# Attention tile: transposed probabilities ahead of the first half of the scores, sink transpose behind it

## The chip, the cores and the metric

The kernel runs on one core of a Trainium2 chip. Its time is the device time of one execution in microseconds (us); lower is better. The core has five engines that run their own instruction queues in order and meet only at semaphores: TensorE (PE; its weight loads are listed apart as PEld), VectorE (DVE), ScalarE (ACT), GpSimd (POOL) and SyncE (SP), which here only starts DMA transfers.

## The reference

Windowed attention with sink keys is followed by a two-level mixture of experts. Batch 4, 8 heads, sequence 768, head width 64, 4 sink keys, window 128; 4 groups of 4 experts with hidden width 1024.

```python
scores = scale * np.matmul(q, k.transpose(0, 1, 3, 2))
keep = is_sink | in_window
scores = np.where(keep, scores, -1000000000.0)
a = np.exp(scores - np.max(scores, axis=-1, keepdims=True))
a = a / (np.sum(a, axis=-1, keepdims=True) + 1e-09)
x = np.matmul(a, v)                       # then reshaped to 3072 x 512
...
g_idx = np.argmax(x @ w_group, axis=1)    # group of a row, then expert in the group
...
h = np.maximum(xg[mask_e] @ w1[g, e], 0.0)
out[tok_idx] = combined[:, None] * (h @ w2[g, e])
```

## The kernel before

All work is written out in program order. `Pinned` (lines 108 to 117) keeps every engine's instructions in the order in which the Python code issues them, so the order of the calls in the loop is the order in each queue; semaphores between the engines follow from which tile an instruction reads and writes. Most instructions are recorded under line 101, the wrapper's, so the profile's rows are told apart by tile names.

**Stages.** The loop of lines 1081 to 1161 runs over i = 0 to 25. It handles 24 attention tiles of 128 query rows (six per batch; t = i mod 6 is the position in the sequence) as a pipeline of three stages. In iteration i, tile i gets its scores, maxima and exponentials; tile a = i - 1 gets its probabilities transposed and multiplied with the values; tile b = i - 2 is brought back to rows, normalized and stored, and its routing logits are computed. Between these lie pieces of the routing (which row goes to which expert) and, from the middle on, the first weight tiles of the experts. After the loop comes the expert stage, matmul after matmul over eleven groups of experts.

**One iteration, PE's queue.** `scores(i, g)` (line 710) fills PSUM tile `ps0` or `ps1` (g = 0 or 1, four heads each) from the keys `kb` and the queries `qb` with 16 matmuls, 64x216, or 64x144 for t = 0. `trans(a)` (line 764) transposes tile a's probabilities `pt` into `tp` with 16 matmuls, heads 0 to 7 in order, each waiting for its own head's exponentials. `sink_t(a)` (line 783) transposes the sink keys' probabilities `sp` with two matmuls, into a part of the PSUM tiles `lg` and `po`. `logits(b)` writes `lg`, `natural(b)` writes `tp`, `values(a, 0)` and `values(a, 1)` add into `po` in four groups of 16 matmuls (`pu` with the previous block's values, then `pa`, for each half of the heads), and `sink_values(a)` adds four more.

**The other queues.** ACT copies `tp` to `pa` (`evac`, line 771, one call for each half of the heads) and `sink_t`'s output to `spT` (`sink_evac`, line 789, two casts), then runs the eight exponentials of `exps(i, 0)` and `exps(i, 1)`, which write `pt`, and at the end `out_evac`, which copies `po` to `xT`. POOL cuts each half of `pa` to the window with two `affine_select` instructions (into `pu` and back into `pa`), four for an iteration, none for t = 0; after the exponentials it makes `sp` (`sink_split`, line 757: two casts and a subtraction). DVE does `maxima(i, g)` (for t > 0 a `copy_predicated` on `ps`, then four fused reductions that give `sm` and `st`), `norm(b)` (reads `tp`, writes `xt`, which SP stores), routing work, and the lower parts `wlo` of the weights. `tp` has one buffer: `trans(a)` of an iteration waits for `norm` of the iteration before. SP starts the store of `xt`, then the next iteration's `vv` (values), then `qb` and `kb` of tile i + 2 after `scores(i, 1)`.

Iterations 0 and 1 fill the pipeline: iteration 1 issues both halves of the scores first, and `warm` adds small matmuls on `lg` after the scores in iterations 0 to 2 (8, 10 and 6). Iterations 24 and 25 have no scores.

Of the kernel before, what the change touches and what calls it, by code (L numbers as in the profile page):

```python
# [130 lines left out]
def moe_attention(tc, kqT, vN, vS, nsw, wgx, w1, w2, out):  # L131
    nc = Pinned(tc)
    v = nc.vector
    with ExitStack() as top, ExitStack() as att:
# [39 lines left out]
        def pair():  # L174
            return ps_p.tile([P, 2, 4 * P], F32, name="tp")

        def warm(k, dst=None):
            dst = pair()[:, 0, 0:192] if k and dst is None else dst
            for _ in range(k):
                nc.tensor.matmul(dst, wz[:, 0:P], wz, start=True, stop=True)  # L180
# [23 lines left out]
        def load_v(i):  # L204
            b, t = divmod(i, NT)
            vts[i] = wk.tile([P, 2, DM], F32, name="vv", bufs=3)
            nc.sync.dma_start(vts[i].rearrange("p f n -> p (f n)"), vN[b, t])
# [15 lines left out]
        def issue():  # L223
            if jobs:
                load(jobs.pop(0))
# [112 lines left out]
        def put_gates(n):  # L338
            for _ in range(min(n, len(gates))):
                t, g = gates.pop(0)  # L340
                nc.sync.dma_start(xd[t * P:(t + 1) * P, DM:XW], g)
# [292 lines left out]
        def gather(r, j):  # L634
            w = min(P, CAPT[r] - j * P)
            cc = BASE[r] + j
            xg[r, j] = t = gp.tile([P, XW], F32, name="xg")
            src = xd[0:sum(BATCHES[:(SNAP if j < EC else SNAPB) + 1]) * P] if r == 0 else xd
            nc.gpsimd.indirect_dma_start(
                out=t[0:w], out_offset=None, in_=src,  # L640
                in_offset=bass.IndirectOffsetOnAxis(ap=gidx[0:w, cc:cc + 1], axis=0))
# [68 lines left out]
        def scores(i, g):  # L710
            t = i % NT
            if g == 0:
                env[i] = e = {}
                e["pt"] = wk.tile([P, H, SW], F32, name="pt", bufs=2)
                if i % 2 == 0:
                    env["st"] = wk.tile([P, 2, 2, H], F32, name="st")
                e["st2"] = env["st"]
                e["st"] = e["st2"][:, :, i % 2]
            m = 3 if t else 2
            for pp in range(2):  # L720
                for j, f in ((0, 0), (1, 1), (0, 1), (1, 0)):
                    d, o = slice(j * D, (j + 1) * D), slice(f * D, (f + 1) * D)
                    end = 2 + 2 * t + f
                    nc.tensor.matmul(psb[g][o, 2 * j + pp, (3 - m) * BW:CW], qb[d, i % NQ, 2 * g + pp, o],
                                     kb[d, end - m:end, 2 * g + pp], start=True, stop=True)
# [4 lines left out]
        def maxima(i, g):  # L730
            t = i % NT
            e = env[i]
            if t:
                v.copy_predicated(psb[g][:, :, CW - D:CW], selu[:, None, :].to_broadcast([P, 4, D]), psb[g][:, :, BW - D:BW])
            e["sm", g] = sm = wk.tile([P, 4, SW], F32, name="sm", bufs=2)
            for k in range(4):
                h = head(g, k)
                v.tensor_tensor_reduce(
                    sm[:, k], psb[g][:, k, CW - SW:CW], msk[:, min(t, 2)], -0.125, 3.0e38,
                    ALU.add, ALU.min, e["st"][:, 0, h:h + 1])  # L740

        def exps(i, g):
            e = env[i]
            for k in range(4):
                h = head(g, k)
                nc.scalar.activation(e["pt"][:, h].rearrange("p (b k) -> p b k", b=2)[:, ::-1],
                                     e["sm", g][:, k].rearrange("p (b k) -> p b k", b=2), AF.Exp, bias=e["st"][:, 0, h:h + 1],
                                     scale=-1.0, accum_out=e["st"][:, 1, h:h + 1])
# [15 lines left out]
        def trans(i):  # L764
            e = env[i]
            for h in range(H):
                for f in range(2):
                    r = slice(f * D, (f + 1) * D)
                    nc.tensor.transpose(env["tp"][:, f, h * D:(h + 1) * D], e["pt"][r, h, NSK:NSK + P], ident[r, r])

        def evac(i, g):
            e = env[i]
            pa = wk.tile([P, 4, P], F32, name="pa", bufs=2)
            nc.scalar.copy(pa.rearrange("p h (f q) -> p f h q", f=2),
                           env["tp"][:, :, 4 * g * D:4 * (g + 1) * D].rearrange("p f (h q) -> p f h q", q=D))
            e["pT", g] = pT = [pa]
            if i % NT:
                for dst, sg in ((pu[g], -1), (pa, 1)):
                    nc.gpsimd.affine_select(out=dst[0:D], in_=pa[0:D], pattern=[[0, 8], [sg, D]], compare_op=ALU.is_ge,
                                            fill=0.0, base=(sg - 1) // 2, channel_multiplier=-sg)  # L780
                pT.append(pu[g])

        def sink_t(i):
            sp = env[i]["sp"].rearrange("p a h k -> p (a h k)").bitcast(F32)
            for f in range(2):
                r = slice(f * D, (f + 1) * D)
                nc.tensor.transpose(ob[f][0:96, 0:D], sp[r], ident[r, r])

        def sink_evac(i):
            env[i]["spT"] = spT = wk.tile([96, P], F32R, name="spT", bufs=2)  # L790
            for f in range(2):
                nc.scalar.copy(spT[:, f * D:(f + 1) * D], ob[f][0:96, 0:D])
# [288 lines left out]
        for i in range(NI + 2):  # L1081
            live = i < NI
            a, b = i - 1, i - 2
            mid, old = 0 <= a < NI, 0 <= b < NI
            state["clk"] += 3.0
            if i == NI:
                state.update(gap=0.0, dve=state["clk"])
                sps.close()
                put_gates(MAXB)
                while later:  # L1090
                    gather(*later.pop(0))
                ps_h = fl.enter_context(tc.tile_pool(name="ps_h", bufs=4, space=PSUM, side="right", reuse_waits="tile"))
                tail.append(ps_h)
                next(ew)
                next(ew)
                if half:
                    half.pop()()()
            if live:
                load_v(i)
            if live:  # L1100
                scores(i, 0)
                if i == 1:
                    scores(i, 1)
            if mid or old:
                env["tp"] = pair()
            if mid:
                trans(a)
                sink_t(a)
                evac(a, 0)
                sink_evac(a)  # L1110
                evac(a, 1)
            if later and not gates:
                gather(*later.pop(0))
            late = None
            if live:
                if i != 1:
                    scores(i, 1)
                issue()
                warm(FILL[i] if i < len(FILL) else 0, ob[0][:, 224:416])
                late = half.pop()() if half else wjob()  # L1120
                if half and i % NT == 0:
                    late = lambda more=half.pop(): more()()
            if live:
                maxima(i, 0)
                exps(i, 0)
            else:
                routing(TSTEP, (None,))
                next(ew, None)
            if old:
                logits(b)  # L1130
                natural(b)
            if live:
                maxima(i, 1)
                exps(i, 1)
                sink_split(i)
            if i == 0:
                late_consts()
            if i % NT == (4 if i else 0) and i < NI - NT + (not i):
                split_s((i + 2) // NT)
            state["clk"] += 3.0  # L1140
            if old:
                norm(b)
            routing(1, ("pe",))
            if old:
                norm_logits(b)
            if late:
                late()
            if mid:
                values(a, 0)
                values(a, 1)  # L1150
                sink_values(a)
                out_evac(a)
            put_gates(2 if live else MAXB)
            routing(UNITS.get(i, REND) if live else TSTEP, (None, "rd"))
            if live and i % 2:
                sums(i)
            if i >= CHOOK and (i % 2 == 0 or i > NI - 4):
                prefetch(min(RAW, len(raws) + (1 if live else RAW)))
            if not live:
                wjob()  # L1160
                next(ew, None)
# [283 lines left out]
```

## Time and profile before

| | us |
|---|---|
| three runs, median | 516.72 |
| lowest and highest of them | 516.55, 520.93 |
| the profiled execution's own time | 515.75 |
| span of its instructions | 514.0 |
| iterations 1 to 23 and the way into the expert stage (12 to 172 us of the span): PE busy | 154.42 of 160.00 |
| expert stage (200 to 514 us): PE busy | 307.46 of 314.00 |
| DVE, ACT, POOL busy in 12 to 172 us | 125.32, 126.78, 77.29 |

A row of the timeline has the start in us from the span's start, the length in us, the engine, the line, the operation, output and inputs, the shape and how many instructions of the kind are merged in the row. A bracket at the end tells how long the engine had stood idle and what released it. Matmuls overlap in the array, so the length of a merged PE row reaches past the start of the next one; the distance from start to start is what a step costs on PE.

The start of `scores(i, 0)` marks an iteration. From iteration 9 to 11 these starts are 59.21, 65.62 and 71.97 us, about 6.35 us apart.

### The profile page before, as it was taken

To read this page: it belongs to the slowest core of one execution; us is meant where nothing else is said; L and a number is where in the kernel's file an instruction comes from. 1 tells how busy PE (TensorE), PEld (TensorE's weight loads), DVE (VectorE), ACT (ScalarE), POOL (GpSimd) and SP (SyncE) were. 2 spreads that over 40 slices of the span, in tenths; PEclk is the share of its full clock that TensorE was granted. 3 is DMA by queue.
4 is the path that set the end of the run, shared out by engine and by line. 5 is a ranking of instruction groups with operands and counts; after the bars stand their busy time and mean duration, and the time that the engine had idled before them with its cause. 6 is when DMAs were issued, how large, how long until landed. Compare 5 with 4: busy or idle time off the path is not lost. (4 is left out here: it accounts for less than half of the span.)

```text
span 514.0 us, 14707 instructions
## 1 busy us (share of the span) xinstructions
PE 497.8 (97%) x5399; PEld 417.6 (81%) x5399; DVE 382.3 (74%) x1183; ACT 345.8 (67%) x901; POOL 157.0 (31%) x272
## 2 busy tenths in 40 slices
PE   7999999999999999999999999999999999999995
PEld 5788888777778888989889868787779788988884
DVE  7566887988997789984175668847888888778840
ACT  4888887878885445772265667845877886687731
POOL 3464452454465011423304021321233032202111
PEclk8999999999999999999999999999999999999999
DMA  7777876797795545996129378859788896869300
GB/s 223 220 212 215 255 216 200 211 299 216 225 306 142 193 122 200 308 302 247 67 93 312 126 270 294 277 181 306 274 254 308 290 313 216 295 213 338 107 24 27
DMA packets 50000, 114.33 MB, mean 222 GB/s; under 512 B 9486, under 2 KB 9486, under 8 KB 49920
## 3 DMA queue, kind: packets, MB, share of 16 engines
q1 hardware_dynamic: 45424, 99.96, 60.6%
q0 software_dynamic: 4352, 13.06, 7.3%
q8 instruction: 44, 0.72, 0.6%
q10 hardware_dynamic: 144, 0.29, 0.2%
q14 instruction: 36, 0.29, 0.2%
HBM read 100.69 MB, written 13.05 MB: 221 GB/s over the span
## 5 line engine op out<-in xcount | busy, mean ns | idle before, releaser
L101 DVE TENSOR_TENSOR wlo<-rw,whi 128x1024 fp32r<-128x1024 f32 x128 | 153.0, 1218 | 38.7 <-ACT whi L101 38.5
L101 PE MATMUL po<-whi,un 128*128 128x512 f32 (+3 forms) x448 | 149.2, 393 | 0.0
L101 ACT CAST whi<-rw 128x1024 fp32r<-128x1024 f32 (+1 forms) x132 | 131.5, 1023 | 16.3 <-DMA rw<-in_w 10.7
L101 PE MATMUL ph<-un,whi 128*128 128x256 f32 (+4 forms) x576 | 132.4, 317 | 0.8 <-DVE hc L101 0.6
L101 POOL DMA_INDIRECT out<-ot,sidx x33 | 45.5, 1380 | 236.7 <-ACT ot L101 143.9
L101 PE MATMUL po<-wlo,un 128*128 128x512 f32 (+4 forms) x264 | 101.6, 390 | 0.0
L101 PE MATMUL ph<-un,wlo 128*128 128x160 f32 (+4 forms) x416 | 100.6, 267 | 0.0
L101 PEld LDWEIGHTS po<-whi,un 128*128 128x128 f32 (+2 forms) x448 | 79.9, 179 | 23.6
L101 PEld LDWEIGHTS ph<-un,whi 128*128 128x128 f32 x576 | 94.7, 189 | 3.3 <-DVE hc L101 1.3
L101 ACT ACTIVATE pt<-sm,st 128x136 f32<-128x136 f32 x192 | 75.8, 406 | 8.7 <-DVE st L101 8.5
L101 PEld LDWEIGHTS ph<-un,wlo 128*128 128x128 f32 x416 | 77.2, 189 | 0.8
L101 PEld LDWEIGHTS po<-wlo,un 128*128 128x128 f32 (+3 forms) x264 | 43.5, 165 | 13.2
L101 DVE CUSTOM_DVE_ANT_0 sm<-ps,msk 128x136 f32<-128x136 f32 x192 | 45.8, 295 | 5.0 <-PE ps L101 0.9
L101 PE MATMUL ps<-kb,qb 64*64 64x216 f32 (+1 forms) x768 | 44.7, 351 | 2.7 <-DMA qb<-in_kqT 2.1
L101 ACT ACTIVATE ot<-po,cg 128x512 f32<-128x512 f32 (+4 forms) x33 | 22.5, 681 | 32.2 <-PE po L101 22.8
L101 POOL DMA_INDIRECT xg<-xd,gidx x33 | 33.4, 1012 | 34.6 <-DVE key L101 22.4
L101 ACT COPY pa<-tp 128x512 f32<-128x512 f32 x48 | 28.5, 593 | 17.4 <-PE po L101 11.0
L101 DVE TENSOR_TENSOR hc<-ph,hc 128x160 f32<-128x160 f32 (+2 forms) x64 | 22.1, 346 | 23.6 <-ACT hc L101 23.5
L101 ACT ACTIVATE un<-ph 128x256 fp32r<-128x256 f32 (+1 forms) x40 | 15.8, 395 | 33.6 <-PE ph L101 33.1
L101 ACT ACTIVATION_READ_ACCUMULATOR pt<-sm,st 128x1 f32 x192 | 37.9, 197 | 0.0
L101 POOL TENSOR_SCALAR_AFFINE_SELECT pu<-pa 64x512 f32<-64x512 f32 x40 | 26.2, 655 | 25.0 <-ACT pa L101 21.4
L101 ACT COPY hc<-ph 128x160 f32<-128x160 f32 (+2 forms) x64 | 19.8, 311 | 19.4 <-PE ph L101 12.4
(190 smaller groups left out, 724.0 us busy)
## 6 DMA issues: line engine op xcount, KB each, us to landing
rw<-in_w SPq DMA_DIRECT2D x128, 512.0 KB, 5.1
vv<-in_vN SPq DMA_DIRECT2D x24, 512.0 KB, 5.2
kb<-in_kqT SPq DMA_DIRECT2D x23, 288.0 KB, 4.0
qb<-in_kqT SPq DMA_DIRECT2D x24, 256.0 KB, 3.6
xd<-xt SPq DMA_DIRECT2D x24, 256.0 KB, 4.1
svr<-in_vS SPq DMA_DIRECT2D x4, 192.0 KB, 3.8
xg<-xd,gidx POOLq DMA_INDIRECT x33, 4.2
out<-ot,sidx POOLq DMA_INDIRECT x33, 4.9
```

The source lines that it names most:

```text
L101: r = f(*a, **k)
```

## The change

In iterations from 2 on, `trans(a)` now comes ahead of `scores(i, 0)`, and `sink_t(a)` behind it. Both `evac` calls follow `trans(a)` directly, and `sink_evac(a)` comes behind both of them, where it stood between them. `scores(i, 1)` and all that follows stay where they were. In iteration 1 both halves of the scores still come first; there only the two `evac` calls and `sink_evac` change places. In iteration 24, without scores, the same. Nothing is computed in another way, and no instruction is added or removed.

```diff
             if live:
                 load_v(i)
-            if live:
+            if i == 1:
                 scores(i, 0)
-                if i == 1:
-                    scores(i, 1)
+                scores(i, 1)
             if mid or old:
                 env["tp"] = pair()
             if mid:
                 trans(a)
+                evac(a, 0)
+                evac(a, 1)
+            if live and i != 1:
+                scores(i, 0)
+            if mid:
                 sink_t(a)
-                evac(a, 0)
                 sink_evac(a)
-                evac(a, 1)
             if later and not gates:
                 gather(*later.pop(0))
```

On PE, iteration 8, from the last matmuls of the iteration before to the logits, before (`ps0` and `ps1` are the two halves of the scores; numbers are buffers):

```order
L101 MATMUL po_198<-spT_1128,svp_783 128x128 x4
L101 MATMUL ps0_195<-kb_88,qb_89 64x216 x8
L101 MATMUL tp_1234<-ident_104,pt_1098 128x64 x16
L101 MATMUL lg_197<-ident_104,sp_1181 96x64
L101 MATMUL po_198<-ident_104,sp_1181 96x64
L101 MATMUL ps1_196<-kb_88,qb_89 64x216 x8
L101 MATMUL lg_197<-wsd_182,xT_1211 64x40 x8
```

and now:

```order
L101 MATMUL po_198<-spT_1130,svp_783 128x128 x4
L101 MATMUL tp_1224<-ident_104,pt_1119 128x64 x16
L101 MATMUL ps0_195<-kb_88,qb_89 64x216 x8
L101 MATMUL lg_197<-ident_104,sp_1181 96x64
L101 MATMUL po_198<-ident_104,sp_1181 96x64
L101 MATMUL ps1_196<-kb_88,qb_89 64x216 x8
L101 MATMUL lg_197<-wsd_182,xT_1211 64x40 x8
```

The transposes of the probabilities and the first half of the scores have changed places; the two sink transposes stand behind the same work as before, in another order.

On ACT, the same iteration, from the copy of the iteration before (`xT`) to the exponentials, before:

```order
L101 COPY xT_1211<-po_198 128x512
L101 COPY pa_1253<-tp_1234 128x2x4x64
L101 CAST spT_1257<-lg_197 96x64
L101 CAST spT_1257<-po_198 96x64
L101 COPY pa_1260<-tp_1234 128x2x4x64
L101 ACTIVATE pt_1224,st_1225<-sm_1275,st_1225 128x2x68 x4
```

and now:

```order
L101 COPY xT_1211<-po_198 128x512
L101 COPY pa_1241<-tp_1224 128x2x4x64
L101 COPY pa_1245<-tp_1224 128x2x4x64
L101 CAST spT_1261<-lg_197 96x64
L101 CAST spT_1261<-po_198 96x64
L101 ACTIVATE pt_1249,st_1250<-sm_1275,st_1250 128x2x68 x4
```

The second copy of `tp` has moved ahead of the two sink casts. The queues of DVE, POOL and SP hold the same rows in the same order as before.

## The prediction

> **What bounds the kernel now.** I read the span and the busy time by stage first, then the waits of the attention stage, then one iteration on every engine.
>
> ```profile
> span 514.0 us, 14707 instructions
> 12.00:172.00 160.00, 154.42 (x3330) 126.91 (x3328) 125.32 (x597) 126.78 (x509) 77.29 (x188) 1.00 0.77 230
> 200.00:514.00 314.00, 307.46 (x1803) 260.35 (x1802) 223.43 (x454) 201.48 (x354) 71.80 (x59) 1.00 0.67 228
> ```
>
> The columns behind the length are PE, PEld, DVE, ACT and POOL. PE bounds both stages, at a granted clock of 1.00: it lacks 160.00 - 154.42 = 5.6 us of being busy throughout in the attention stage. The change touches that stage alone; since PE is as full in the expert stage (307.46 of 314.00), what attention gains or loses should arrive at the end. As 1% of 516.72 is 5.2 us, about what a measurement of this kernel can tell from no change, the edit would have to remove nearly every gap of PE to be seen as faster.
>
> The waits of 12 to 172 us (who waits, for whom, us in total, times, longest):
>
> ```profile
> PEld lg L101 <- POOL sp L101: 2.5, 7, 0.5
> PEld tp L101 <- ACT pt L101: 2.1, 6, 0.5
> PEld po L101 <- POOL pa L101: 1.4, 8, 0.2
> PE lg L101 <- POOL sp L101: 1.2, 4, 0.4
> PE po L101 <- issue: 1.0, 1, 1.0
> PE lg L101 <- ACT spT L101: 0.9, 3, 0.6
> ```
>
> Three waits repeat: the last group of value matmuls for POOL's fourth cut (`po <- POOL pa`), the sink transposes for POOL's copies (`lg <- POOL sp`), and the transposes of the probabilities for the exponentials (`tp <- ACT pt`). The change moves the first and the third; I show that the second stays.
>
> One ordinary iteration, PE first:
>
> ```profile
> 65.62 0.96 PE L101 MATMUL ps<-kb,qb 64*64 64x216 f32 x16
> 66.52 0.71 PE L101 MATMUL tp<-ident,pt 64*128 64x64 f32 x16
> 67.06 0.22 PE L101 MATMUL lg<-ident,sp 64*96 64x64 f32 x1
> 67.21 0.96 PE L101 MATMUL ps<-kb,qb 64*64 64x216 f32 x16
> ...
> 69.09 0.69 PE L101 MATMUL po<-pu,vv 128*64 128x64 f32 x16
> 69.61 0.64 PE L101 MATMUL po<-pa,vv 128*64 128x64 f32 x16
> 70.08 0.65 PE L101 MATMUL po<-pu,vv 128*64 128x64 f32 x16
> 70.76 0.69 PE L101 MATMUL po<-pa,vv 128*64 128x64 f32 x16
> ...
> 71.97 0.41 PE L101 MATMUL ps<-kb,qb 64*64 64x216 f32 x4
> ```
>
> From start to start, half a set of scores costs 66.52 - 65.62 = 0.90 us, the transposes 0.54, the sink pair 0.15. The value groups step by 0.52, 0.47 and 0.68: the last is 0.21 over the step before it. The iteration takes 6.35 us.
>
> The same iteration on ACT, POOL and DVE:
>
> ```profile
> 65.79 0.59 ACT L101 COPY xT<-po 128x512 f32<-128x512 f32 x1 [0.42 <-PE po L101]
> 67.35 0.59 ACT L101 COPY pa<-tp 128x512 f32<-128x512 f32 x1 [0.77 <-PE lg L101]
> 68.04 0.60 ACT L101 COPY pa<-tp 128x512 f32<-128x512 f32 x1
> 68.52 0.43 ACT L101 ACTIVATE pt<-sm,st 128x136 f32<-128x136 f32 x1
> 71.27 0.41 ACT L101 ACTIVATE pt<-sm,st 128x136 f32<-128x136 f32 x1
> 68.01 0.65 POOL L101 TENSOR_SCALAR_AFFINE_SELECT pu<-pa 64x512 f32<-64x512 f32 x1 [2.00 <-ACT pa L101]
> 70.06 0.65 POOL L101 TENSOR_SCALAR_AFFINE_SELECT pa<-pa 64x512 f32<-64x512 f32 x1
> 66.65 0.43 DVE L101 COPY_PREDICATED ps<-selu,ps 128x256 f32<-128x256 int32 x1 [0.47 <-PE ps L101]
> 67.12 0.30 DVE L101 CUSTOM_DVE_ANT_0 sm<-ps,msk 128x136 f32<-128x136 f32 x1
> 69.58 0.69 DVE L101 TENSOR_TENSOR xt<-tp,rc 128x512 f32<-128x512 f32 x1
> ```
>
> POOL's four cuts start when the first `pa` copy is done and end at 70.71, and PE's last group starts at 70.76: that chain sets the 0.21.
>
> **The change part by part.**
>
> *Transposes first.* They start at 65.62 instead of 66.52 and end 0.71 later, at 66.33. The first `pa` copy started 0.12 behind their end (67.35 against 67.23), so now at 66.45; `xT`, ahead of it on ACT, ends at 66.38 and leaves it that. So all four cuts come 0.90 us earlier; the last ends at 69.81, where PE would want it at 70.08 + 0.47 = 70.55. The 0.21 goes, in the 8 iterations of the wait row: 8 x 0.21 = **-1.7 us**. What is late next there is PE itself.
>
> *Both `pa` copies ahead of the casts, the casts ahead of the exponentials.* The second copy no longer waits for casts. After an iteration with short scores the logits wait for a cast:
>
> ```profile
> 80.54 0.67 PE L101 MATMUL lg<-wsd,xT 128*64 128x40 f32 x16 [0.16 <-ACT spT L101]
> ```
>
> With the ACT chain 0.9 us earlier, even the cast behind two copies comes in time. The wait row has 0.9 us in three places, the longest 0.56 (the start, below); the other two give **-0.3 us**.
>
> *First half of the scores later by 0.54.* DVE's `copy_predicated` moves from 66.65 to 67.2, the first maximum from about 67.4 to 67.95. The exponentials began at 68.52 because ACT was busy until then; now ACT is free at about 68.0 and DVE ready at 67.95, so they begin near 68.05, 0.47 us earlier. The second half of the scores keeps its place, since the sum of what stands ahead of it is the same. `norm` moves by some 0.4 us, from an end of 70.27 to 70.7; the next transposes, which need its buffer, want it at 71.97, so 1.3 us of cover are left where there were 2.2. Behind `norm` SP's store and the load of `vv` slip by the same 0.4; that load
>
> ```profile
> vv<-in_vN SPq DMA_DIRECT2D x24, 512.0 KB, 5.2
> ```
>
> takes 5.2 us and is read more than a whole iteration later (6.35 us), so it stays hidden. `qb` and `kb` follow the second half of the scores, which does not move. Cost: nothing.
>
> *Sink transposes behind the scores.* They stand behind the same 0.90 + 0.54 us of work in either order, at 67.06. Their wait for POOL (2.5 us by the weight loads' row) is for `sp`, made after the last exponential; at an unmoved end of the exponentials it stays as it is. The earlier end could shorten it: I take 0 and keep 2.5 as the far end.
>
> *Transposes without the scores as cover.* Their last pair needs the last head's exponentials. That was covered by 0.90 us of scores. Where ACT is behind PE, the wait now comes ahead of the scores and the second half gets later. The iteration at 130.18 shows it:
>
> ```profile
> 130.18 0.96 PE L101 MATMUL ps<-kb,qb 64*64 64x216 f32 x16
> 131.87 0.26 PE L101 MATMUL lg<-ident,sp 64*96 64x64 f32 x1
> 130.69 0.39 ACT L101 ACTIVATE pt<-sm,st 128x136 f32<-128x136 f32 x1
> 131.24 0.35 POOL L101 CAST sp<-pt 128x32 fp32r<-128x32 f32 x2 [6.27 <-ACT pt L101]
> 127.14 0.42 DVE L101 COPY_PREDICATED ps<-selu,ps 128x256 f32<-128x256 int32 x1
> ```
>
> The waiting cast on POOL starts at 131.24, so the last head is ready then; the last pair and what follows it go to about 131.36, the scores to 132.25, and the sink pair starts there instead of at 131.87: 0.38 later. The exponentials of that iteration's predecessor hang on DVE, which reached `ps` only at 127.14 behind routing work and a weight tile, not on PE, so this end does not come earlier. It happens where an iteration without cuts (t = 0), short on PE, precedes: three places in the loop, of which the first has little routing in front of it. Two times 0.38: **+0.8 us**.
>
> *The start.* In iteration 1 the warming matmuls follow the first sink cast:
>
> ```profile
> 12.85 0.99 PE L101 MATMUL lg<-wz 128*128 128x192 bf16 x10 [0.56 <-ACT spT L101]
> 12.59 0.21 ACT L101 CAST spT<-lg 96x64 fp32r<-96x64 f32 x1
> 16.02 0.41 ACT L101 ACTIVATE pt<-sm,st 128x136 f32<-128x136 f32 x1
> 17.27 0.26 PE L101 MATMUL lg<-ident,sp 64*96 64x64 f32 x1 [0.24 <-POOL sp L101]
> ```
>
> With a second `pa` copy (a step of 0.48) ahead of the cast, they begin 0.48 later. Iteration 2's transposes then end 0.18 behind the exponentials (16.02 + 0.41 + 0.1), at 16.7, the scores at 17.6, and the sink pair starts there instead of at 17.27: **+0.3 us**.
>
> Sum: -1.7 - 0.3 + 0.8 + 0.3 = **-0.9 us**. The profiled execution, 515.75 us for a span of 514.0, would go to 514.85. The median of the runs stands 0.97 above that execution; I predict against the median: **515.8 us**.
>
> **The rivals.**
>
> *More is gained.* If the exponentials end 0.47 earlier also where ACT is behind, the +0.8 goes and the sinks' 2.5 us with it: -1.7 - 0.3 + 0.3 - 2.5 = -4.2, 512.5 us. For it: the ACT chain is shorter in every iteration. Against it: at 127.14 DVE, not ACT, sets the exponentials.
>
> *The gain is swallowed.* Iterations 17 to 21 hang on a chain of weight tile, routing, maxima and exponentials; if that chain starts as late as before, the gain ahead of it becomes waiting, and only losses count: 516.7 to 517.8 us. Against it: the chain itself hangs on iteration 17's scores, which come earlier.
>
> *Every iteration waits for the exponentials, and the change is slower.* The transposes are exposed as soon as the last exponential ends more than 0.54 - 0.18 = 0.36 us behind the start of an iteration. It now ends at 71.27 + 0.5 = 71.77 for a start of 71.97, 0.2 ahead; with the scores 0.54 later for DVE, and if ACT gained nothing, it would end 0.34 behind, at the very point. Were all 21 full iterations to pay the 0.38 of the one shown: 21 x 0.38 = 8 us, less 2.0 and with the 0.3 of the start: +6.3, 523.0 us. Against it: ACT idles 0.77 us ahead of its first `pa` copy, and that idling is what the change removes.
>
> *POOL is held by DVE.* One sink cast shows what a collision costs:
>
> ```profile
> 144.58 1.21 POOL L101 CAST sp<-pt 128x32 fp32r<-128x32 f32 x1
> ```
>
> It ends with the weight tile `wlo` that DVE runs at that time, where the pair of casts at 131.24 takes 0.35. There are four such tiles in the stage, and DVE's work moves 0.4 us back, `sp` 0.5 forward; a collision more in two of them costs at most 2 x 1.2 less the gain: -0.9 + 2.4, 518.2 us. [...]
>
> **How the numbers follow.** Forecast 0.62 (514.6 to 517.0), more gained 0.12, swallowed 0.10, POOL held 0.06, every iteration exposed 0.10, most of it at a part of the full price. The range takes in the first four cases but the outer half of the gains and the larger prices of exposure: **513.3 to 518.3 us**. Faster by over 1% (below 511.6) needs more than the full second case, with the single gap of 1.0 us at "issue" too: 0.06. Slower by over 1% (above 521.9) needs exposure at nearly its full price, or a new wait that no row shows: 0.08. Within 1%: 0.86.
>
> **What would show it.** In the changed profile: the wait `po <- POOL pa` gone; the first `pa` copy about 0.8 us behind an iteration's start, not 1.7; PE's iterations near 6.1 us where they were 6.35; the wait of `tp` for `pt` grown on PE only in the iterations after a t = 0 one; the warming matmuls at 13.3; the same length from the end of attention to the last instruction. The forecast is wrong if `tp <- ACT pt` appears in most iterations, if DVE's `norm` releases the transposes, or if the iterations shorten and the expert stage starts no earlier.

## The result and the profile after

The changed kernel takes 521.93 us (median of 14 runs), the kernel before, run beside it, 516.52 us (14 runs): a ratio of 1.008, 95% interval 1.0052 to 1.0107, so by the interval 2.7 to 5.5 us slower. Two of the 14 runs, 525.67 and 784.9 us, were slow ones and stand outside the ratio. The forecast was 515.8 us with a range up to 518.3. The profiled execution of the changed kernel took 522.76 us for a span of 521.0.

The span and the busy times of the two stages (columns as before: PE, PEld, DVE, ACT, POOL, clock) of the changed kernel:

```profile
span 521.0 us, 14733 instructions
12.00:172.00 160.00, 149.88 (x3259) 121.83 (x3255) 125.80 (x591) 125.29 (x505) 75.86 (x189) 1.00 0.73 218
200.00:514.00 314.00, 314.00 (x1838) 266.26 (x1837) 230.15 (x477) 205.47 (x358) 68.31 (x60) 1.00 0.68 230
```

PE lacks 160.00 - 149.88 = 10.1 us of being busy throughout in the attention stage, where it lacked 5.6. The clock is 1.00 in both stretches, so what PE lacks here went into waits. The waits of 12 to 172 us that matter (who waits, for whom, us in total, times, longest):

```profile
ACT pt L101 <- DVE st L101: 18.2, 18, 3.2
PEld tp L101 <- ACT pt L101: 3.6, 9, 0.7
PE po L101 <- POOL sp L101: 1.8, 1, 1.8
PE tp L101 <- DVE xt L101: 1.7, 4, 0.6
PE lg L101 <- DVE af L101: 1.1, 1, 1.1
PE lg L101 <- DVE tab L101: 0.9, 1, 0.9
```

The wait `po <- POOL pa` is gone, as forecast. In its place stand waits for DVE (`xt`, `af`, `tab`), exponentials that wait for DVE's maxima 18 times, and one of 1.8 us put down to POOL's `sp` which, as the experiments bear out, is none for POOL at all.

One ordinary iteration on PE now (start, length, what):

```profile
72.96 0.67 PE L101 MATMUL lg<-wsd,xT 128*64 128x40 f32 x16
74.94 0.64 PE L101 MATMUL po<-pu,vv 128*64 128x64 f32 x16
75.40 0.64 PE L101 MATMUL po<-pa,vv 128*64 128x64 f32 x16
75.97 0.66 PE L101 MATMUL po<-spT,svp 96*128 96x128 f32 x4
76.56 0.72 PE L101 MATMUL tp<-ident,pt 64*128 64x64 f32 x16
77.21 0.96 PE L101 MATMUL ps<-kb,qb 64*64 64x216 f32 x16
78.10 0.26 PE L101 MATMUL lg<-ident,sp 64*96 64x64 f32 x1
78.29 0.96 PE L101 MATMUL ps<-kb,qb 64*64 64x216 f32 x16
79.18 0.67 PE L101 MATMUL lg<-wsd,xT 128*64 128x40 f32 x16
```

The last value group starts 0.46 behind the third (0.68 before): the 0.21 went. But the transposes now cost 77.21 - 76.56 = 0.65 to the next start, where they cost 0.54 in front of the sink pair, and that pair 0.19 where it cost 0.15. The iteration takes 79.18 - 72.96 = 6.22 us where it took 6.35.

I read the loss by iteration, at the start of the logits (`lg<-wsd,xT`). Of the 7.0 us between the two profiled spans, the changed kernel is 1.8 behind at iteration 2 (20.72 against 18.96), loses 3.1 from there to 13, wins 1.5 back to 18, and loses 3.0 in the step from 18 to 19; 0.9 come behind that, and the expert stage gives back 0.2. About 1.0 of the 1.8 is the first scores of the loop, which took longer in this execution (before, then after); the second execution of the changed kernel has 1.21 us for them again:

```profile
6.25 1.21 PE L101 MATMUL ps<-kb,qb 64*64 64x144 f32 x32 [2.12 <-DMA qb<-in_kqT]
6.41 2.20 PE L101 MATMUL ps<-kb,qb 64*64 64x144 f32 x32 [2.22 <-DMA qb<-in_kqT]
```

The step from 18 to 19 before and, below, after:

```profile
120.43 0.67 PE L101 MATMUL lg<-wsd,xT 128*64 128x40 f32 x16
127.52 0.67 PE L101 MATMUL lg<-wsd,xT 128*64 128x40 f32 x16
```

```profile
123.79 0.67 PE L101 MATMUL lg<-wsd,xT 128*64 128x40 f32 x16
126.47 0.54 PE L101 MATMUL lg<-af,bf 128*128 128x112 f32 x3 [1.15 <-DVE af L101]
132.78 0.23 PE L101 MATMUL lg<-ident,sp 64*96 64x64 f32 x1 [0.87 <-DVE tab L101]
133.86 0.67 PE L101 MATMUL lg<-wsd,xT 128*64 128x40 f32 x16
```

7.09 us became 10.07, with DVE waited for. DVE and POOL around that place in the kernel before (`rss` and `svp` belong to iteration 16):

```profile
110.16 0.17 DVE L101 TENSOR_SCALAR rss<-rs 128x12 f32<-128x12 f32 x1
111.47 1.27 POOL L101 TENSOR_TENSOR svp<-svr,svp 32x512 fp32r<-32x512 f32 x1
117.29 1.22 DVE L101 TENSOR_TENSOR wlo<-rw,whi 128x1024 fp32r<-128x1024 f32 x1
118.42 0.52 DVE L101 TENSOR_TENSOR af<-oh,av 128x336 fp32r<-128x336 bf16 x1
118.86 0.56 DVE L101 TENSOR_TENSOR bf<-colm,ga 128x384 fp32r<-128x384 f32 x1
119.82 0.16 DVE L101 TENSOR_SCALAR rc<-st 128x16 f32<-128x16 f32 x1
119.95 0.65 POOL L101 TENSOR_SCALAR_AFFINE_SELECT pu<-pa 64x512 f32<-64x512 f32 x1 [0.42 <-PE po L101]
```

and in the changed kernel:

```profile
115.49 1.27 POOL L101 TENSOR_TENSOR svp<-svr,svp 32x512 fp32r<-32x512 f32 x1
115.70 1.09 DVE L101 TENSOR_SCALAR rss<-rs 128x12 f32<-128x12 f32 x1
122.53 1.22 DVE L101 TENSOR_TENSOR wlo<-rw,whi 128x1024 fp32r<-128x1024 f32 x1
123.14 1.12 POOL L101 TENSOR_SCALAR_AFFINE_SELECT pu<-pa 64x512 f32<-64x512 f32 x1 [0.47 <-ACT pa L101]
123.67 0.95 DVE L101 TENSOR_TENSOR af<-oh,av 128x336 fp32r<-128x336 bf16 x1
124.54 1.00 DVE L101 TENSOR_TENSOR bf<-colm,ga 128x384 fp32r<-128x384 f32 x1
125.46 0.95 DVE L101 TENSOR_TENSOR af<-oh,av 128x336 fp32r<-128x336 bf16 x1
126.33 0.62 DVE L101 TENSOR_SCALAR rc<-st 128x16 f32<-128x16 f32 x1
```

Before, DVE was done with `af`, `bf`, `af`, `rc` when POOL's first cut began, 0.48 us ahead of the logits at 120.43. Now it reaches the weight tile `wlo` 1.26 us ahead of the logits (123.79 - 122.53) where it was 3.14 ahead (120.43 - 117.29), and all four operations run beside the cuts, and both sides take longer: `af` 0.52 to 0.95, `bf` 0.56 to 1.00, `rc` 0.16 to 0.62, the cuts 0.65 to between 0.80 and 1.12 (the first of them already beside `wlo`). In iteration 16 `rss` took 1.09 us instead of 0.17 and ended with POOL's `svp`.

### The profile page after: what moved, and what is told of

It reads as the page before. It is cut to its first block, busy times and chain, and to the rows that moved or that the text cites. A ratio compares the mean times of both kernels' runs of the same rounds, so it can differ in the third digit from the quotient of the medians.

```text
span 521.0 us, 14733 instructions
## 1 busy us (share of the span) xinstructions
PE 499.8 (96%) x5399; PEld 419.4 (80%) x5399; DVE 386.1 (74%) x1183; ACT 347.6 (67%) x901; POOL 151.7 (29%) x272
## 2 busy tenths in 40 slices
DMA packets 50002, 114.34 MB, mean 219 GB/s; under 512 B 9487, under 2 KB 9487, under 8 KB 49921
## 3 DMA queue, kind: packets, MB, share of 16 engines
q1 hardware_dynamic: 45424, 99.96, 59.7%
## 5 line engine op out<-in xcount | busy, mean ns | idle before, releaser
L101 POOL DMA_INDIRECT out<-ot,sidx x33 | 41.5, 1257 | 241.4 <-ACT ot L101 138.1
L101 PE MATMUL ps<-kb,qb 64*64 64x216 f32 (+1 forms) x768 | 46.4, 359 | 2.6 <-DMA qb<-in_kqT 2.2
L101 ACT ACTIVATION_READ_ACCUMULATOR pt<-sm,st 128x1 f32 x192 | 36.3, 189 | 0.0
L101 PEld LDWEIGHTS ps<-kb,qb 64*64 64x64 f32 x768 | 26.0, 139 | 9.6 <-issue 3.4
L101 PE MATMUL po<-pa,vv 128*64 128x64 f32 x768 | 30.5, 223 | 2.5 <-POOL sp L101 1.8
L101 POOL TENSOR_SCALAR_AFFINE_SELECT pu<-pa 64x512 f32<-64x512 f32 x40 | 27.6, 690 | 17.8 <-ACT pa L101 17.6
```

Source lines behind the costliest of these rows:

```text
L101: r = f(*a, **k)
```

## The experiments

**Two more executions.** First, both kernels again without an edit, to see what returns.

> The kernel before, unchanged, for a second profile. Theory A (the order makes DVE late in iterations 14 to 22): the span is 514 us within 1 us, PE's gaps at issue are at other places than in the first profile and add up to 1 to 3 us, and DVE's af and bf instructions take about 0.5 us each. Theory B (the loss is made of one-off gaps at the start and at issue that differ from execution to execution): the second span differs from the first by 2 us or more.

> The changed kernel, unchanged, for a second profile. Theory A: the jump of about 3 us in iteration 18 and the waits of the transposes for DVE xt (1.7 us in the first profile) come again at the same places; the gap of 1.9 us in iteration 6 and the 1.4 us at the start need not. Theory B: iteration 18 loses nothing this time, and other gaps stand elsewhere.

Measured: 519.7 us and 520.32 us, one execution each, beside 516.85 us for the median of 13 runs before. In the changed kernel the step from 18 to 19 was 10.08 us (10.07 in the first profile), in the kernel before 7.09 again; `rss`, `af`, `bf`, `rc` took the same lengths to 0.01 us as in its first profile. That part belongs to the order. The spans don't show it: 518.0 us for the kernel before, 4.0 above its first profile as theory B had it, and 518.5 for the changed one. Waits of 0.2 to 1.8 us of PE in value groups, most of them with no releaser ("issue"), were of another size in every execution of both kernels: those are the part that varies.

**The change in halves.** Run a3 has the new order on PE alone, a4 the new order on ACT alone.

Against the changed kernel (a3) and against the kernel before (a4):

```diff
                 trans(a)
                 evac(a, 0)
-                evac(a, 1)
...
                 sink_t(a)
                 sink_evac(a)
+                evac(a, 1)
```

```diff
                 sink_t(a)
                 evac(a, 0)
+                evac(a, 1)
                 sink_evac(a)
-                evac(a, 1)
```

> PE in the order of the changed kernel, ACT in the order of the kernel before (first copy of tp, the two sink casts, second copy). Theory A: the scores' first half is late for DVE as in the changed kernel, so it is slower than before by 3 to 6 us; the second copy comes behind the sink transposes, so the exponentials start later by up to 0.5 us more. Theory B: no difference from before beyond 1 us.

> PE in the order of the kernel before, ACT in the order of the changed kernel (both copies of tp, then the two sink casts). Theory A: DVE gets its scores as early as before, so no loss in iterations 14 to 22; the start pays 0.3 us and short iterations get their logits later by some 0.2 us: within 1.5 us of before. Theory B: within 1 us of before as well. If this one is slower by 3 us or more, the order of ACT and not that of PE makes the loss.

Measured: a3 523.06 us, ratio 1.0117 (1.005 to 1.0183); a4 519.62 us, ratio 1.0052 (1.0029 to 1.0076). Neither half gains; a4, expected within 1.5 us of before, is a miss. In a4 the logits wait 0.40 us for ACT's sink cast in nearly every iteration (6.55 us for an ordinary one): the cast behind both copies is late when the transposes aren't early. In a3 the iterations are 6.21 us as in the changed kernel, and the step from 18 to 19 is 7.09: behind a wait of 1.92 us and 10 us at a granted clock of 0.50 DVE was ahead there.

**Where along the loop.** b1 has the old order in iteration 18 alone, b2 from 13 on; b3 takes out POOL's cuts in iteration 18; b4 moves `norm` ahead in the four iterations where `xt` releases the transposes.

```diff
 b1: old order where i == 18       b2: old order where i > 12
 b3: -  for dst, sg in ((pu[g], -1), (pa, 1)):
     +  for dst, sg in ((pu[g], -1), (pa, 1)) if i != 17 else ():
 b4: +  if i in (14, 17, 19, 21):
     +      norm(b)                 (ahead of maxima(i, 1))
```

> Theory C: the lasting part of the loss is made in one iteration, 18, where POOL's four cuts of tile 17, drawn ahead by the new order, run at the same time as DVE's routing operations with two SBUF inputs and lengthen them (0.5 to 0.95 us), so that DVE reaches the maxima late and PE waits. With the old order in iteration 18 alone the step from iteration 18 to 19, 3.0 us longer than before in the changed kernel, is 1 us or less longer, and the kernel comes within -0.5 to +2 us of the kernel before. Theory D: DVE is late on its own from iteration 14 on because the first half of the scores reaches it 0.55 us later in each of them; then one iteration in the old order only moves the loss to a neighbour, and the kernel stays 3 us or more above before. Theory B: the loss is in one-off gaps of PE; the step is as it falls.

> New order in iterations 2 to 12 only. Theories C and D both put the loss behind iteration 13, so: iterations 3 to 12 some 0.1 us shorter each, nothing lost behind; 0.2 to 1 us faster than before. Theory B (gaps of PE that the new order makes larger in the first twelve iterations, +4.2 us to iteration 9 in the first profile of the changed kernel): 2 us or more slower than before.

> New order throughout; POOL's four cuts of tile 17, in iteration 18, are left out, so tile 17 is computed without the cut of its window on the left and right blocks. Theory C: DVE's three routing operations of iteration 18 go back from 0.95-1.00 to 0.50-0.55 us, the cuts being what held them, and the step from iteration 18 to 19 is at most 1.2 us longer than before, where the changed kernel has 3.0. Theory D: the step stays 2.5 us or more longer.

> New order; in iterations 14, 17, 19 and 21 DVE runs norm ahead of the second half of the maxima. If norm is what releases the transposes in iterations 15, 18, 20 and 22 (0.58, 0.17, 0.41 and 0.58 us in the profiles of the changed kernel), those four waits go and up to 1.7 us is gained against the changed kernel. Rival: the second half of the exponentials then comes some 0.7 us later and is what the transposes wait for, so the waits change their name and nothing is gained.

Measured: b1 523.26 us, ratio 1.0127 (1.0074 to 1.018): the step from 18 to 19 is 7.37 us, but the time is above the range that theory C gave, and not below the changed kernel's. In its profile a wait of 2.18 us in iteration 17 had held the cuts back until DVE was done, so the edit wasn't tested. b2 519.85 us, ratio 1.006 (1.0026 to 1.0095): a miss, slower by 3 us although the order is the old one where the collision stands; theory C can't be all. b3: `af`, `bf`, `af`, `rc` went back to 0.49, 0.55, 0.50 and 0.16 us, as C says; its step (9.3 us) can't be read, since PE's clock stood at 0.50 from 123.5 to 133.8 us, and its time neither, since the rest of its span took 396 us where the others take 344. b4 524.63 us, ratio 1.0168 (1.0097 to 1.0239): the rival was right, in three of the four places the wait became `tp <- ACT pt` (0.51 where `xt` had 0.58), in the fourth `xt` stayed at 0.42, and nothing was gained.

**The waits without a releaser.** The trace holds every packet of the DMA queues. Its queue q8, of the kind "instruction", moved 0.74 MB in 45 packets in the changed kernel, each of 16384 bytes. The first of these waits in the changed kernel, and the queue's line for the stretch 47.1 to 47.2 us:

```profile
49.53 0.69 PE L101 MATMUL po<-pa,vv 128*64 128x64 f32 x16 [1.83 <-POOL sp L101]
```

```profile
q8 instruction: 1, 0.02, 61.7%
```

The packet runs from 47.14 to 48.12, and PE goes on 1.41 us later. No other one came between 42.0 and 47.1, while q1, which moved 99.96 of the execution's 114.34 MB, kept the 16 engines busy (packets, MB, share of 16 engines in that stretch):

```profile
q1 hardware_dynamic: 479, 1.17, 81.7%
```

Over the profiles of the 18 kernel executions, PE has 60 waits of 0.3 us or more between 15 and 172 us that are put down to "issue", or in a value group to `sp`; every one ends 1.22 to 1.66 us behind the end of such a packet. I read them as PE's waits for its own instructions ("fetch waits" below). So I moved the loads (c1, c2) and the instructions (c3, c4).

```diff
 c1 (new order), c2 (old order):
-            if live:
+            if live and i < 2:
                 load_v(i)
 ...
                 issue()
+                if 0 < i < NI - 1:
+                    load_v(i + 1)
 ...        (vv bufs=3 -> 4, xt bufs=2 -> 1)
 c3 (new order), c4 (old order):
         warm(WARM)
+        for _ in range(20):
+            nc.tensor.matmul(pair()[:, 0, 0:32], wz[:, 0:P], wz[:, 0:32], start=True, stop=True)
```

> New order; SP starts the load of vv about 2 us earlier, right behind qb and kb of the iteration before (four buffers for vv, one for xt to make room). Theory E: the 3 us that the new order loses between iterations 2 and 13 are waits of PE for its own instruction fetches (packets of 16 KB on queue q8), which stand in the transfer engines behind the loads; in the new order xt's store and vv start 0.4 to 0.7 us later against PE's program, so the fetches that fall there come later. With vv moved away the gaps of PE in iterations 5 to 10 (3.6 and 2.7 us in the two profiles of the changed kernel) fall to under 1 us and the kernel is about 2 to 3 us faster than the changed kernel: 518 to 520 us. Rival: the fetches queue behind whatever is under way, since the transfer engines are busy three quarters of the time; then the gaps move or stay and the time stays at 521 to 523 us.

> The same edit in the old order, as the control of the run beside it. Theory E: the old order has gaps of 0 to 1 us there, so little to gain: within 1 us of the kernel before. Rival: the load now meets fetches that it did not meet, and gaps of 1 us or more appear: 1 to 3 us slower.

> New order with 20 small matmuls (32 columns of zeros, some 0.1 us each) behind the first 18 warming matmuls, where PE waits 2.1 us for the first load: everything behind stands 40 instructions later in PE's stream, and nothing else changes. Theory E: the places of the gaps are bounds between fetched blocks, so the gap of iteration 6 moves from the start of the fourth group of value matmuls to some 20 matmuls ahead of it, inside the second group, and the one of iteration 8 likewise; sizes change with it. Rival F: the gaps are a wait for data (the names in the profile are POOL's sp and, once, vv); then they stay at the start of the fourth group.

> The same 20 small matmuls in the old order. Theory E: the bounds move by 20 matmuls here too (gaps at the fourth group of iterations 6, 8 and 16 in the profiles of the kernel before would stand in the second), and how large the gaps are is a matter of where the bounds fall against the loads: 1 to 4 us to either side of the kernel before would show that the order of the program is not needed for such a loss. Rival F: no change beyond 0.5 us.

Measured: c1 526.56 us (1.0137, 1.008 to 1.0193), c2 524.19 us (1.0106, 1.0053 to 1.016), c3 524.31 us (1.0126, 1.0076 to 1.0175), c4 518.49 us (1.0013, 0.998 to 1.0045). Moving `vv` took away the wait of iteration 6 but not that of iteration 8 (1.29 us), and cost both orders more than either theory said. The one buffer for xt has a part in it: `norm` waits for the store of the `xt` before (2.2 us in two places in c1, 4.3 in five in c2), and in iteration 16 DVE stands idle ahead of `xt` for 1.97 us in c1 and 2.05 in c2, which the other profiles don't have. c4 can't be told from the kernel before. c3 bears out that the waits follow the place in PE's stream, not the data: nothing of it in iterations 6 and 8, and one of 0.80 us in the last value group of iteration 4; d1, below, has the same order up to there and a wait in iteration 6 (the second row):

```profile
38.25 0.34 PE L101 MATMUL po<-pa,vv 128*64 128x64 f32 x4 [0.80 <-issue]
49.84 0.34 PE L101 MATMUL po<-pa,vv 128*64 128x64 f32 x4 [1.12 <-issue]
```

Counted in PE's matmuls from the program's start, the waits of the two profiles of the changed kernel up to iteration 9 come behind matmul 724, 850, 976, 1102 and 1228, 126 apart. Those of c3, d1 and d2 come behind 598 and 850, on the same count; as 20 of these are the added ones, d1's wait stands inside the second group of iteration 6, where theory E put it. c3 and d2 have only the one two blocks ahead of it.

The 20 matmuls aren't free: they step by 0.24 us, not 0.1, and the first scores start at 8.92 us in c3 and c4 instead of 5.96 to 6.41. So c3 is to be held against c4: 1.0126 against 1.0013, and the new order loses with the new places too. c2, in the old order, shows the collision too, with a step from 18 to 19 of 11.48 us, partly at a granted clock of 0.50: what loses there is the meeting of DVE and POOL, whatever makes DVE late (in c2, its wait for the store).

**Both causes out.** The same 20 matmuls in b1's and b2's orders, and PE's wait in iteration 18 filled with work on zeros.

```diff
 d1 = b1 + c3's lines      d2 = b2 + c3's lines
 d3: natural(b)
     +  if i == 18:
     +      warm(7, ob[0][:, 224:416])
```

> New order but in iteration 18, with the 20 small matmuls at the start. Collision and fetches as the causes: no step of 3 us from iteration 18 to 19, and the fetch gap of 2.2 us that the form without the 20 had in iteration 17 elsewhere or smaller; 517 to 520 us, some 3 to 5 us below the same form without the 20 (523.3) and below the new order with the 20 (524.3). Rival: the new order costs in every iteration from 13 on, whatever the fetches do: 522 us or more.

> New order in iterations 2 to 12, old order behind, with the 20 small matmuls. Fetches as the cause of the 3 us that this form lost without the 20: gaps of PE in iterations 5 to 10 under 1 us instead of 3.1, and within 1.5 us of the old order with the 20 (517.0 to 520.0). Rival: the new order itself loses in these iterations: 521 us or more.

> New order throughout, with 7 matmuls of zeros on PE ahead of the three routing matmuls of iteration 18, where PE waits 1.15 us for DVE. The chain through DVE is not touched, so the step from iteration 18 to 19 stays 2.5 us or more above that of before. If idling there is what halves PE's clock behind it (2 of 3 profiles of this order, 3.4 to 10.2 us long, each worth half its length), the clock stays at 1.00 between 120 and 145 us and the median falls by 1 to 3 us against the changed kernel (521.9): 519 to 521. Rival: the halved clock has other causes, or comes with the later waits: 521 to 524 us and still windows at half clock.

Measured: d1 525.91 us (1.016, 1.0117 to 1.0202), a miss: without the wait that had helped b1, DVE was late all the same, its operations met the cuts in the old order too, and the step was 9.63 us. What makes DVE late therefore stands ahead of iteration 18. d2 520.23 us (1.0048, 1.0023 to 1.0074), a little over its range, with no collision; c4, the old order with the same 20, has 1.0013, and their intervals overlap. d3 522.51 us (1.0099, 1.0068 to 1.0131), a miss: the clock stayed at 1.00 in the profile, but the time didn't fall; as fetch waits of 0.33 and 0.54 us ahead of it had put DVE further ahead, with two of the four operations spared (step 7.81), it doesn't settle the clock's part.

**The first meeting.** In the changed kernel `rss` beside `svp`, in iteration 16, is where DVE falls behind. e1 moves `svp` one iteration ahead.

```diff
-            if i % NT == (4 if i else 0) and i < NI - NT + (not i):
-                split_s((i + 2) // NT)
+            if i == 15 or i % NT == (4 if i else 0) and i < NI - NT + (not i) and i != 16:
+                split_s((i + 3) // NT)
```

> New order; the split of the sink values of the fourth batch (ACT's copy and POOL's svp of 1.27 us) in iteration 15 instead of 16. If the first collision is what makes DVE late enough for the second, rss takes 0.17 us again, DVE starts the weight tile wlo some 1 us sooner than 1.26 us ahead of iteration 18's logits, at most two of the four operations af, bf, af, rc are lengthened, and the step from iteration 18 to 19 is 7.1 to 8.5 us instead of 10.1; the median falls by 1 to 3 us against the changed kernel (521.9): 519 to 521. Rival: DVE is late by the later scores alone, the cuts still meet all four, and the step stays at 9.6 to 10.1 us.

Measured: 520.51 us, ratio 1.0069 (1.0037 to 1.01). The rows of DVE, and the logits of iterations 18 and 19, in e1:

```profile
112.89 0.17 DVE L101 TENSOR_SCALAR rss<-rs 128x12 f32<-128x12 f32 x1
119.37 1.25 DVE L101 TENSOR_TENSOR wlo<-rw,whi 128x1024 fp32r<-128x1024 f32 x1
120.54 0.49 DVE L101 TENSOR_TENSOR af<-oh,av 128x336 fp32r<-128x336 bf16 x1
```

```profile
123.32 0.67 PE L101 MATMUL lg<-wsd,xT 128*64 128x40 f32 x16
130.34 0.66 PE L101 MATMUL lg<-wsd,xT 128*64 128x40 f32 x16
```

`rss` is short again, none of the four is lengthened, and the step is 7.02 us. A fetch wait of 1.62 us in iteration 17 helped by that much: without it `wlo` would begin 2.3 us ahead of the logits instead of 3.95, against 1.26 in the changed kernel. So the first meeting costs DVE about 1.1 us. That none of the four is held is in part the fetch wait's doing: in d3 `wlo` began 2.65 us ahead, and two of them were lengthened. In time e1 can't be told from the changed kernel, whose interval overlaps its own.

Side by side, worked out from the traces (us; "fetch" is the sum of PE's waits that end 1.2 to 1.7 us behind a q8 packet, "rest" what is left without them):

```
                        iterations 2 to 13        step       ratio to before
                        length  fetch   rest    18 to 19
before                  68.47   0.00   68.47      7.09
before again (a1)       70.02   1.05   68.97      7.09
old, 20 small (c4)      68.65   0.00   68.65      7.30        1.0013
changed                 71.60   2.53   69.07     10.07        1.0080
changed again (a2)      71.20   2.69   68.51     10.08
changed, 20 small (c3)  69.42   0.80   68.62     10.92        1.0126
new to 12 (b2)          71.69   3.12   68.57      7.30        1.0060
new to 12, 20 small(d2) 69.19   0.80   68.39      7.09        1.0048
svp ahead (e1)          69.91   1.28   68.63      7.02        1.0069
```

Two things can be read from it. Without the fetch waits the new order gains nothing in iterations 2 to 13: 68.4 to 69.1 us against 68.5 to 69.0. And it has more of them there: without the 20 matmuls 1.28 to 3.12 us, 2.4 on average, in seven profiles (b3 left out), where the old order has 0 and 1.05; with them 0.80, 0.80 and 1.37 where it has 0. Which half of the change brings them isn't clear: a3, the new order on PE alone, has 3.14, and a4, the new order on ACT alone, 1.70. Over all of iterations 2 to 25 the two orders don't differ in this: 2.4 and 3.6 us in the two profiles of the kernel before, 3.0 and 3.2 in those of the changed one.

## Why the prediction was wrong

**"Transposes first: -1.7 us."** The wait went, as said, but the gain was mis-sized by a cost that I had taken as fixed. A step's price on PE depends here on what follows it: transposes in front of scores 0.65 us instead of 0.54, the sink pair between two halves of the scores 0.19 instead of 0.15. Iterations with the wait went from 6.35 to 6.21 us; those without it grew, from iteration 2 to 3 from 6.07 to 6.21 and from 7 to 8 from 5.46 to 5.66. Without the fetch waits the sum over iterations 2 to 13 is zero. I had read both step prices from the old order, where that very pair of neighbours didn't occur.

**"First half of the scores later by 0.54. Cost: nothing."** This is the step that failed. It counted cover in one ordinary iteration (1.3 us for `norm`), left out DVE's routing work, which iterations 13 to 18 have besides, and took the end of the exponentials, behind which POOL's work starts, as unmoved. Counted from the logits of iteration 16 (106.26 us before, 111.56 after), the first `copy_predicated` comes 0.50 us later and `rss` 0.24, but the last exponential ends 0.99 sooner (3.10 us behind the logits instead of 4.09) and `svp` starts 1.28 sooner. So `rss`, which had been done 1.14 us ahead of `svp`, now starts 0.21 behind its start. DVE's later work and POOL's earlier work together bring the first meeting; it costs DVE another microsecond, and four operations come to lie beside the cuts: 3.0 us more in the step from 18 to 19. `norm` releases the transposes in four iterations (0.58, 0.17, 0.41 and 0.58 us, 1.7 in all), a price where the prediction had none, and which the prediction had named as a sign of being wrong.

**The rival "POOL is held by DVE"** had a collision of the two engines, but the wrong partners: it priced `wlo` against `sp` and gave the four cuts no price. In an ordinary iteration of the changed kernel three of them (at 72.57, 73.18 and 73.90 us) lie beside the maxima and take 0.65 us each, as before. In iteration 18 they lie beside DVE's routing, and the meeting costs about 3 us: the step is 9.63 to 11.48 us in the six profiles with three or four lengthened operations (10.07 and 9.63 in the changed kernel and d1, which are at a clock of 1.00 there, the other four partly at 0.50), and 7.02 to 7.81 in eleven of the others (the twelfth, b3's, can't be read). What decides is how far ahead of iteration 18's logits `wlo` begins: 1.04 to 1.26 us in the six, 2.65 in d3 (7.81), 3.13 to 4.65 in the other ten. The first meeting is one way to be late, not the only one: c1 and c2 have the second without it (`rss` 0.32 and 0.54 us, clear of `svp`), behind their waits for the store. What the collision is worth in the kernel's time isn't shown: e1, without it, is no faster beyond the intervals.

**"Transposes without the scores as cover: +0.8."** Right in kind: `tp` waits for `pt` on PE only behind the short iterations, 0.31 and 0.22 us where I had 0.38 twice; at the third place, iteration 20, DVE's `xt` is waited for instead. The rival that exposes every iteration is out.

**"The start: +0.3."** The warming matmuls wait 1.22 us for the sink cast instead of 0.56, 0.66 more where I had 0.48, but 0.68 in the second profile, 0.12 more. It can't be read in the span: the logits of iteration 2 came 1.76 us later than before in one profile and 0.25 sooner in the other.

**What no term held** are the fetch waits. The page of the kernel before shows them as a single `po <- issue` of 1.0 us, which the prediction quoted and left aside. In the new order 2.5 us of them fall into iterations 2 to 13, where PE has nothing else to wait for; before, they fell behind iteration 13 (2.4 us in its first profile), where in the changed kernel DVE is the one that is late; that DVE could use them there is argued, not shown. Why the new order has more of them in its first half stays open: in iterations 2 to 10 xt's store and `vv` start up to 0.6 us later against PE's logits, but moving `vv` didn't settle it. So does the split of the whole loss: b2 puts 0.6% on the new order up to iteration 12, d2 beside c4 0.35% with overlapping intervals, and what the collision adds in the executions that have it can't be told within these intervals.

## What to carry to other kernels

Price a moved step with the neighbours that it gets, and look for a row with that pair before taking its old price. When a change makes one engine's work earlier and another's later, lay the two engines' rows side by side in the fullest iterations, not in an ordinary one: here the ordinary iteration came out as forecast to about 0.1 us, and the one step that lost 3 us in both profiles lies where DVE has routing work as well. A wait named "issue", or one whose named releaser had long been done, is worth a look at the instruction queue's packets.

## What the runs showed of the hardware

In the 18 profiles PE stood 60 times for 0.3 us or more, up to 2.7, until 1.22 to 1.66 us behind the end of a packet of queue q8. The packets are of 16384 bytes, 25 of them between 15 and 172 us in the changed kernel and 26 in the kernel before, about one in 6 us. That PE waits there for its instructions is my reading. The places went by the position in PE's stream: with 20 matmuls more ahead of it, the wait in the last value group of iteration 6 was gone in c3 and stood in the second group in d1 (1.12 us). The size was not fixed by it: behind matmul 850 the new order without the 20 matmuls waited 1.01 to 2.64 us in eight profiles, and not at all in c1, where `vv` had moved. What sets the time of a packet is not shown; q1 stood at 81.7% ahead of the first.

In c3 PE's granted clock was 0.50 for about 10 us behind waits for DVE of 1.15 and 0.88 us in iterations 18 and 19 (columns as above, the clock third from the end):

```profile
132.00:136.00 4.00, 4.00 (x52) 2.84 (x54) 3.60 (x24) 2.87 (x15) 0.00 (x0) 0.50 0.86 293
136.00:140.00 4.00, 4.00 (x56) 3.54 (x57) 3.46 (x11) 1.62 (x6) 0.57 (x3) 0.50 0.70 193
```

The step from iteration 19 to 20 took 8.79 us there, 5.90 in the changed kernel, whose clock stayed at 1.00 behind the same two waits (1.15 and 0.87). In the attention stage ten of the 18 profiles have such stretches, 3.41, 6.83 or 10.24 us long, with waits of 0.7 to 2.7 us ahead of them. Which waits are followed by one stays open.
